# Attention, gated MLP and output projection in one kernel: PV products two at a time in the Wo part, Wo matmuls in blocks of two steps, and other first steps

## The chip, the cores and the metric

The kernel runs on one core of a Trainium2 chip. The metric is the time of the device in microseconds (us); a time is the median of its runs, and next to it stands one profiled execution, from which every duration below is taken. A core has a tensor engine (PE for its matmuls, PEld for its weight loads, which overlap the matmuls), a vector engine (DVE), a scalar engine (ACT), GpSimd (POOL), and SyncE (SP), which issues nearly all DMA transfers here.

## The reference

One block with 2048 tokens of 512 features, an attention with 32 heads of 16 features, and an MLP of width 1376 whose result is the gate of the attention's output:

```python
xn = layernorm(x)                                   # (1, 2048, 512)
q, k, v = split(xn @ wqkv)                          # 32 heads, 16 wide
p = softmax(q k^T / 4)
s = (p v) @ wo
g = silu(gelu_tanh(xn @ w1 + b1) @ w2 + b2)
out = x + s * g
```

## The kernel before

The kernel has three parts. The first, up to about 470 us, makes the layernorm, the transposes, q, k and v and the MLP, each float32 product as three matmuls of split operands; between these matmuls it makes the first 580 of 2048 score tiles that only serve the row maximum ("S tiles"). The second part, which the change touches, is a loop of steps n = 0 to 512. The third, from about 1531 us to the end, makes the Wo product of the last six token tiles.

A step belongs to a unit (four heads by 512 queries; 32 units of 16 steps, so that a step is one unit by 128 keys). It consists of

- four T tiles (`t_one`, L713): transposed scores, 128 keys by 512 queries, one per head. Each uses 64 of the array's rows, so two run side by side; they go to four PSUM banks (`ps`, the two halves of `two`, `pst`), and ACT makes their exponentials in three instructions (L716 for `ps`, L718 for both halves of `two`, L716 for `pst`);
- one PV product V (`pv_step`, L784) of the step before: four matmuls on column tiles (128 rows by 32 columns) that the trace shows as eight records. After the 16th of a unit DVE copies the result out (`os`, L791), `o_move` (L804, L807) sends it on, and `o_den` and `o_div` (L813, L816, L822) divide it by the sums;
- up to three S tiles (L192 on PE, then a maximum on DVE, L198), written S for a whole tile and X and Y for the two halves of one that is cut. They use three banks in a ring. `due(n)` says how many S tiles stand by step n: three a step, but two in the first step (k = 0) of the first `FEW` units after the first. When a unit's 64 are done, DVE (L243, L254), POOL (L245, L246) and four small transfers (L275) put its maxima in memory, and `load_mh` (L162) reads them back as rows of the T tiles' operands;
- or, once S is finished (from step `DONE`), two Wo half products H (`w_halves`, L911). Token tiles 0 to 9 go in five pairs (t, t + 1), four steps a pair. H multiplies one 128-row block k of the attention's output by Wo, for both tokens of the pair at once on the upper and the lower 64 rows ("side" tells which token has which half): three matmuls for each token, which run in pairs, the last pair with the low part `ol`.

The letters of a step's order are written out in strings: `ORDER[3]` = "XTSTTYSTV" with three S tiles, `FIRST` for the first step of a unit with three. For H, other work is hooked behind the n-th T tile. A pair's other work is hooked in the same way: `load_gx` (L840, L841, on SP) loads g and x of a token to one of four `gx` buffers, or to freed places; `w_two` makes the high and low parts of two 128-row blocks of both tokens (ACT L889 high, the very first on POOL L891; POOL L892 low); `gate` is a tanh on ACT (L845) and a product on DVE (L846); `w_out` multiplies the Wo result by the gate (DVE L917), adds x on POOL (L922) and issues the store on SP (L923).

Of the kernel before, what the change touches and what calls it, by code (L numbers as in the profile page):

```python
# [19 lines left out]
H = 32  # L20
# [12 lines left out]
LEAD = 144  # L33
NW = 10
EARLY = 4
DONE = 492
FILL0 = 30
APART = 5
HB = 4
W2B = 2  # L40
ORDER = {0: "TTTTV", 2: "TSTTSTV", 3: "XTSTTYSTV"}
FIRST = "SXTTTSYTV"
SOON = 580
FEW = 4
SIDES = ((1, 1), (0, 0), (0, 1), (1, 0))
HC = CH // 2
PAIRED = 26
# [6 lines left out]
def fused(ctx: ExitStack, tc: tile.TileContext, x, wqk, wv, wo, w1, b1, w2, b2, out):  # L54
    nc = tc.nc
# [47 lines left out]
    def s_tile(held=False):  # L103
        pool = s_ring.pop(0)
        if not held:
            s_ring.append(pool)
        return pool.tile([P, CH], F32, name="ps"), pool
# [64 lines left out]
    def tick():  # L172
        for e in later:
            e[0] -= 1

    def flush():
        while later and later[0][0] <= 0:
            u = later.pop(0)[1]
            s_send(u)
# [5 lines left out]
    def s_mm(ps, job, a, c0, k0, w):  # L185
        u, st, p = job
        qi, ki = at_of(job)
        if u not in MX:
            MX[u] = qring.tile([P, GH, NCH, NCH, 2], F32, name="mx")
        r = slice(64 * a, 64 * a + 3 * DH)  # L190
        k0 += ki * CH
        return nc.tensor.matmul(ps[:, c0:c0 + w], QS[u][r, p, qi * P:(qi + 1) * P],  # L192
                                kts[u // NCH % KB][p][r, k0:k0 + w], start=True, stop=True).ins

    def s_max(ps, job, heads, parts):
        u, p = job[0], job[2]
        qi, ki = at_of(job)
        nc.vector.tensor_reduce(MX[u][:, 2 * p:2 * p + 2, qi, ki][:, heads, parts], ps.rearrange("p (n c) -> p n c", c=HC), axis=AX.X, op=OP.max)  # L198
        done[u] += 1
        if done[u] == 64:  # L200
            ended.append(u)
            if u == NU - 1:
                s_end0(u)

    def s_whole(job, a):
        ps = s_tile()[0]
        s_mm(ps, job, a, 0, 0, CH)
        s_max(ps, job, a, slice(0, 2))
# [7 lines left out]
    def s_op(op):  # L216
        if op == "S":
            if whole:
                s_whole(whole.pop(), 1)
            else:  # L220
                whole.append(jobs.pop(0))
                s_whole(whole[0], 0)
        elif op == "X":
            if not cut:
                cut[:] = [jobs.pop(0), 0]
            ps, pool = s_tile(True)
            x = s_mm(ps, cut[0], 0, 0, cut[1] * HC, HC)
            cut[2:] = [ps, pool, x]
        else:
            job, n, ps, pool, x = cut  # L230
            hold = nc.tensor.nop().ins
            tc.add_manual_dep(hold, x.name, SYNC, reason="row tile done")
            s_mm(ps, job, 1, HC, n * HC, HC)
            s_max(ps, job, slice(0, 2), n)
            s_ring.append(pool)
            cut[1] += 1
            if n:
                cut.clear()

    def s_turn(u, nm):  # L240
        later.append([8 if u == NU - 1 else 12, u])
        nt = qring.tile([P, 2 * GH * NCH], F32, name="nt")
        nc.vector.transpose(nt, nm)  # L243
        mh = MH[u] = qring.tile([P, 2, 2 * GH * NCH], F32R, name="mh")
        nc.gpsimd.tensor_copy(mh[:, 0], nt)  # L245
        nc.gpsimd.tensor_sub(mh[:, 1], nt, mh[:, 0].bitcast(F32))  # L246

    def s_end0(u):
        ended.remove(u)
        us = units_of(u)  # L250
        w = u % 2 * GH * NCH
        nm = nms[u // 2 % 2]
        mx = MX.pop(u).rearrange("p a b c n -> p (a b) (c n)")
        nc.vector.tensor_reduce(nm[:, w:w + GH * NCH], mx, axis=AX.X, op=OP.max, negate=True)  # L254
        if u == us[-1]:
            if "seen" in prog or u == NU - 1:
                s_turn(us[0], nm)
            else:
                put_off.append((us[0], nm))
        del QS[u]  # L260
        if "seen" in prog:
            ask_qs(u + 2)
        else:
            load_qs(u + 2)
# [45 lines left out]
    for j in range(len(pairs)):  # L310
        for h in range(2):
# [9 lines left out]
            n = 2 if nd < len(parts) and parts[nd][2] and ready - nd > room else 1  # L321
            n = max(n, need - 2 * (left - 1))
            while nd < ready and n > 0:
                c, f, k = parts[nd]
# [453 lines left out]
    def pv_step(u, k):  # L778
        g = u // NCH
        if k == 0:  # L780
            PV[u] = ps_v.tile([P, CH], F32, name="pv")
        for j in range(GH):
            h = (g * GH + j) * VW
            nc.tensor.matmul(PV[u][32 * j:32 * j + 32, :], vsb[:, k, h:h + 32], PT[u, k][:, j, :],  # L784
                             start=(k == 0), stop=(k == NT - 1))
        del PT[u, k]
        if k == NT - 1:
            OS[u] = wb.tile([P, CH], F32, name="os", bufs=1)
            pv = PV.pop(u)
            if u < NU - 1:  # L790
                nc.vector.tensor_copy(OS[u], pv)  # L791
            else:
                nc.scalar.activation(OS[u][:, :HC], pv[:, :HC], AF.Copy)
                nc.vector.tensor_copy(OS[u][:, HC:], pv[:, HC:])
# [104 lines left out]
    def w_halves(t, k, side):  # L899
        ts = (t, t + 1)  # L900
        if k == 0 and side == 0:
            for i in ts:
                PW[i] = [s_tile()[0]]
        elif k % 2 == 0:
            hold = nc.tensor.nop().ins
            tc.add_manual_dep(hold, HALF[0].name, SYNC, reason="row tile done")
        for n, (x, y) in enumerate(((0, 0), (0, 1), (1, 0))):
            for a in range(2):
                i = ts[a ^ side]
                r = slice(64 * a, 64 * a + 64)  # L910
                HALF[0] = nc.tensor.matmul(PW[i][0], OTS[i, k][x][r], (wo_h, wo_l)[y][r, k],  # L911
                                           start=k == 0 and side == 0 and n == 0,
                                           stop=k == KT - 1 and side == 1 and n == 2).ins
# [15 lines left out]
    todo = {}  # L929

    def at(n, f, *a, pos=3):
        todo.setdefault((n, pos), []).append((f, a))
# [4 lines left out]
    def due(n):  # L937
        return min(4 * L, SOON + max(0, 3 * n - 1) - min(FEW, n // 16))

# [21 lines left out]
    for t in range(NW):  # L961
        n = DONE + 4 * (t // 2)
        at(n - 3 + t % 2, load_gx, t)
        if t % 2 == 0:
            for i in range(4):
                if i % 2 == 0:
                    at(n + i - 2, w_two, t, i)
                for j in range(2):
                    at(n + i, w_halves, t, i // 2 * 2 + j, i % 2, pos=1 + 2 * j)
        at(n + t % 2, gate, t)  # L970
        at(n + 3, w_out, t, nc.gpsimd)
    for i, t in enumerate(late):
        n = L - 2 * len(late) - 1 + 2 * i
        at(n - 4, load_gx, t)
# [9 lines left out]
    for n in range(L + 1):  # L984
        ua, ka = divmod(n, 16)
        want = due(n) - due(n - 1)
        i = 0
        if put_off and ka > 1:
            s_turn(*put_off.pop(0))
        else:  # L990
            for u in list(ended):
                if u >= PAIRED or ka > 2 and since.setdefault(u, n) < n:
                    s_end0(u)
        order = ORDER[want] if n > 1 else ("TTTTV", "TSTTSVT")[n]
        if want == 3 and ka == 0:
            order = FIRST
        for op in order:
            if op in "SXY":
                s_op(op)
            elif op == "V":  # L1000
                if n:
                    pv_step(*divmod(n - 1, 16))
                for _ in range(4):
                    tick()
                flush()
            else:
                if EARLY <= 4 * n + i < 4 * L:
                    t_one(ua, ka, i, True)
                for f, args in todo.get((n, i), []):
                    f(*args)  # L1010
                i += 1
# [54 lines left out]
```

## Time and profile before

| | |
|---|---|
| median of three runs | 1554.22 us (1554.19 to 1554.6) |
| the profiled execution | 1554.05 us, span 1552.3 us |
| granted TensorE clock | 1.00 |
| busy: PE, DVE, ACT, POOL | 1544.9, 1415.1, 1214.2, 367.7 us |
| steps with three S tiles (V to V) | 2.01 to 2.02 us each |
| first steps of units with three S tiles | about 1.21 us from V's end to the next V, where another step has 1.02 |
| steps with two H | 3.04 to 3.05 us |
| V of step 491 to V of step 512 (21 steps) | 1467.14 to 1530.07 us |

Busy times are sums over the instructions of an engine; PE's records overlap (two tiles side by side), so its share says that PE always has something, not how much of the array works. A row of the timeline gives start, duration, engine, line, output and input, and the number of instructions that were put together. The gap that counts for a step is that between the starts of two V.

### The profile page before, as it was taken

The page shows a single profiled execution, that of the slowest core. Times are in us where ns is not written, and L with a number is a line of the kernel's source. Part 1 is how long each engine was busy: PE and PEld are TensorE (multiplying, and loading weights), DVE is VectorE, ACT ScalarE, POOL GpSimd, SP SyncE. Part 2 cuts the span into 40 slices and gives each one's busy share as a digit, 9 for nine tenths or more (in the row PEclk, how much of TensorE's full clock was granted, in tenths as well). Part 3 has the DMA queues.
Part 4 walks back from the last instruction along what each step waited for, and adds up shares of the span by engine and source line. Part 5 has one row for each costly group of instructions (what it writes and reads, how often), then busy time and mean ns, then how long its engine had stood idle before and what let it go on. Part 6 is the DMA issues. An engine that isn't in the chain of part 4 may idle for free.

```text
span 1552.3 us, 31308 instructions
## 1 busy us (share of the span) xinstructions
PE 1544.9 (100%) x12242; PEld 926.8 (60%) x12242; DVE 1415.1 (91%) x2295; ACT 1214.2 (78%) x1881; POOL 367.7 (24%) x370
## 2 busy tenths in 40 slices
PE   9999999999999999999999999999999999999999
PEld 8899999999994444444444444444444444444455
DVE  7599999999998999999999999999999999999834
ACT  4333433434339999999999999999999999999984
POOL 4145675765741001001000100100010000000143
PEclk9999999999999999999999999999999999999999
DMA  6625443454422113113311411411041111110153
GB/s 211 154 60 146 129 140 100 145 152 122 130 85 77 44 36 67 30 37 61 66 28 30 70 37 36 69 34 29 23 81 29 33 30 32 41 30 22 48 197 115
DMA packets 78643, 116.83 MB, mean 75 GB/s; under 512 B 28036, under 2 KB 28292, under 8 KB 77320
## 3 DMA queue, kind: packets, MB, share of 16 engines
q1 hardware_dynamic: 74748, 101.89, 23.8%
q0 software_dynamic: 3264, 12.35, 4.7%
q8 instruction: 96, 1.57, 0.4%
q10 hardware_dynamic: 484, 0.60, 0.1%
q14 instruction: 51, 0.42, 0.1%
HBM read 84.35 MB, written 25.97 MB: 71 GB/s over the span
## 4 chain that ended last, share of the span: by engine, by line
PE 98%; DVE 1%; DMA 0%; ACT 0%; issue 0%; DVEq 0%
PE pv L784 33%; PE ps L192 22%; PE ps L582 13%; PE two L713 8%; PE sp L582 5%; PE pst L713 4%; PE ps L713 4%; PE pst L582 3%; PE pv L582 2%; PE ps L911 2%; PE ps L91 1%; PE ps L454 1%; PE pst L91 0%; DVE st L413 0%; PE two L91 0%; DMA xt<-in_x 0%
## 5 line engine op out<-in xcount | busy, mean ns | idle before, releaser
L198 DVE TENSOR_REDUCE mx<-ps 128x2 f32<-128x512 f32 x2048 | 1318.5, 687 | 75.3 <-PE ps L192 25.8
L784 PE MATMUL pv<-slot,vsb 128*32 128x512 f32 x4096 | 545.4, 605 | 0.9 <-DVE os L791 0.9
L718 ACT ACTIVATE slot<-two 128x1024 f32<-128x1024 f32 x511 | 520.4, 1018 | 4.3 <-PE pst L713 3.7
L192 PEld LDWEIGHTS ps<-kt,slot 48*128 48x128 f32 x1364 | 214.2, 185 | 295.8 <-DVE mx L198 285.0
L192 PE MATMUL ps<-kt,slot 48*128 48x256 f32 (+1 forms) x1364 | 374.8, 364 | 0.0
L716 ACT ACTIVATE slot<-ps 128x512 f32<-128x512 f32 x515 | 307.1, 597 | 18.0 <-PE ps L713 6.6
L716 ACT ACTIVATE slot<-pst 128x512 f32<-128x512 f32 x511 | 309.5, 606 | 0.6 <-PE ps L713 0.6
L582 PE MATMUL ps<-slot,w1h 64*128 64x512 f32 x1088 | 222.9, 393 | 0.0
L713 PE MATMUL two<-qt,kt 50*128 50x512 f32 x766 | 202.4, 399 | 0.3 <-DVE gt L642 0.3
L192 PE MATMUL ps<-kt,qz 48*128 48x512 f32 x512 | 202.5, 396 | 0.0
L713 PE MATMUL ps<-qt,kt 50*128 50x512 f32 x387 | 190.4, 494 | 0.0
L192 PEld LDWEIGHTS ps<-slot,slot 48*128 48x128 f32 x594 | 93.7, 184 | 126.3 <-DVE mx L198 121.5
L192 PE MATMUL ps<-slot,slot 48*128 48x256 f32 (+1 forms) x594 | 164.8, 364 | 0.0
L582 PEld LDWEIGHTS ps<-slot,w1h 64*128 64x128 f32 x1088 | 155.0, 186 | 8.8
L784 PEld LDWEIGHTS pv<-slot,vsb 128*32 128x32 f32 x4096 | 80.9, 108 | 131.0 <-issue 121.4
L582 PE MATMUL ps<-slot,w1l 64*128 64x512 f32 x544 | 155.1, 393 | 0.0
L713 PE MATMUL pst<-qt,kt 50*128 50x512 f32 x383 | 154.9, 405 | 0.0
L367 ACT ACTIVATE hg<-ps,b_sb 128x512 f32<-128x512 f32 x44 | 27.9, 684 | 134.7 <-PE ps L582 123.3
L374 POOL TENSOR_TENSOR hl<-hg,hh 128x512 fp32r<-128x512 f32 x76 | 96.8, 1296 | 153.2 <-ACT hh L373 107.4
L713 PEld LDWEIGHTS two<-qt,kt 50*128 50x128 f32 x766 | 114.8, 186 | 2.6 <-DVE gt L642 0.7
L245 POOL CAST mh<-nt 128x32 fp32r<-128x32 f32 x19 | 4.0, 209 | 394.0 <-DVE nt L243 329.3
L192 PEld LDWEIGHTS ps<-kt,qz 48*128 48x128 f32 x512 | 93.9, 183 | 0.9 <-DVE mx L198 0.6
(194 smaller groups left out, 1954.5 us busy)
## 6 DMA issues: line engine op xcount, KB each, us to landing
raw<-in_w SPq DMA_DIRECT2D x88, 256.0 KB
qk_h<-hh SPq DMA_DIRECT2D x32, 256.0 KB
qk_l<-hl SPq DMA_DIRECT2D x32, 256.0 KB
qt<-qk_h SPq DMA_DIRECT2D x128, 64.0 KB
slot<-qk_h SPq DMA_DIRECT2D x92, 64.0 KB
g_d<-gt POOLq DMA_DIRECT2D x16, 256.0 KB, 3.6
qt<-qk_l SPq DMA_DIRECT2D x64, 64.0 KB
dn<-den_d SPq DMA_DIRECT2D x32, 128.0 KB
```

The costliest lines, as they stand in the source:

```text
L91: nc.tensor.matmul(ps, lhs[a], rhs[b], start=first and n == 0, stop=last and n == 2)
L192: return nc.tensor.matmul(ps[:, c0:c0 + w], QS[u][r, p, qi * P:(qi + 1) * P], kts[u // NCH % KB][p][r, k0:k0 + w], start=True, stop=True).ins
L198: nc.vector.tensor_reduce(MX[u][:, 2 * p:2 * p + 2, qi, ki][:, heads, parts], ps.rearrange("p (n c) -> p n c", c=HC), axis=AX.X, op=OP.max)
L367: nc.scalar.activation(raw, ph.pop(u), AF.Gelu_apprx_tanh, bias=b1_sb[:, u[2]:u[2] + 1])
L374: nc.gpsimd.tensor_sub(hl, raw, hh.bitcast(F32))
L454: nc.tensor.matmul(pq["q", g, c], W1[g][i][:, k * P:(k + 1) * P], (xh, xl)[j][c][:, k], start=n == 0 and k == 0, stop=n == 2 and k == KT - 1)
L582: i = nc.tensor.matmul(ps, lhs[r], rhs[r], start=first, stop=last).ins
L713: nc.tensor.matmul(ps, kts[g % KB][p][r, k * P:(k + 1) * P], QT[u][r, p, :], start=True, stop=True)
L716: nc.scalar.activation(PT[u, k][:, 2 * p + a, :], ps, AF.Exp, scale=SCALE)
L718: nc.scalar.activation(PT[u, k][:, :2], TP["two"], AF.Exp, scale=SCALE)
L784: nc.tensor.matmul(PV[u][32 * j:32 * j + 32, :], vsb[:, k, h:h + 32], PT[u, k][:, j, :], start=(k == 0), stop=(k == NT - 1))
L911: HALF[0] = nc.tensor.matmul(PW[i][0], OTS[i, k][x][r], (wo_h, wo_l)[y][r, k], start=k == 0 and side == 0 and n == 0, stop=k == KT - 1 and ...
```

## The change

In the Wo part the four T tiles of a step now stand together, and so do the H products, and V is made in even steps only, for the two steps before at once. So a block of two steps reads "TTTTHH" and "HTTTTHVV". The order in which H goes through the blocks k and the sides changes: side 0 of all four blocks first, then side 1, so that one PE wait per pair (the `hold` no-op) is left of the three. `w_two` of a pair's first and second half stand two and one step ahead of the pair. `w_out` stands at the letter W. S ends one step later, since `FEW` goes from 4 to 7: the first steps of units 5, 6 and 7 (n = 80, 96, 112) have two S tiles in place of three, and each S tile after that stands up to three tiles later. Wo starts at step 493 and its last H stand in step 512. In the first steps with three S tiles the first T tile stands ahead of X. New line numbers are one higher (L714 for L713 and so on).

```diff
--- before.py
+++ after.py
@@ -33,15 +33,16 @@
 LEAD = 144
 NW = 10
 EARLY = 4
-DONE = 492
+DONE = 493
 FILL0 = 30
 APART = 5
 HB = 4
 W2B = 2
 ORDER = {0: "TTTTV", 2: "TSTTSTV", 3: "XTSTTYSTV"}
-FIRST = "SXTTTSYTV"
+FIRST = "STXTTSYTV"
+TWO = ("HTTTTHWV", "TTTTHHV")
 SOON = 580
-FEW = 4
+FEW = 7
 SIDES = ((1, 1), (0, 0), (0, 1), (1, 0))
 HC = CH // 2
 PAIRED = 26
@@ -901,7 +902,7 @@
         if k == 0 and side == 0:
             for i in ts:
                 PW[i] = [s_tile()[0]]
-        elif k % 2 == 0:
+        elif k == 0:
             hold = nc.tensor.nop().ins
             tc.add_manual_dep(hold, HALF[0].name, SYNC, reason="row tile done")
         for n, (x, y) in enumerate(((0, 0), (0, 1), (1, 0))):
@@ -962,13 +963,13 @@
         n = DONE + 4 * (t // 2)
         at(n - 3 + t % 2, load_gx, t)
         if t % 2 == 0:
+            for i in range(2):
+                at(n + i - 2, w_two, t, 2 * i)
             for i in range(4):
-                if i % 2 == 0:
-                    at(n + i - 2, w_two, t, i)
                 for j in range(2):
-                    at(n + i, w_halves, t, i // 2 * 2 + j, i % 2, pos=1 + 2 * j)
+                    at(n + i, w_halves, t, i % 2 * 2 + j, i // 2, pos="H")
         at(n + t % 2, gate, t)
-        at(n + 3, w_out, t, nc.gpsimd)
+        at(n + 3, w_out, t, nc.gpsimd, pos="W")
     for i, t in enumerate(late):
         n = L - 2 * len(late) - 1 + 2 * i
         at(n - 4, load_gx, t)
@@ -991,15 +992,22 @@
             for u in list(ended):
                 if u >= PAIRED or ka > 2 and since.setdefault(u, n) < n:
                     s_end0(u)
-        order = ORDER[want] if n > 1 else ("TTTTV", "TSTTSVT")[n]
+        order = TWO[n % 2] if n >= DONE else ORDER[want] if n > 1 else ("TTTTV", "TSTTSVT")[n]
         if want == 3 and ka == 0:
             order = FIRST
         for op in order:
             if op in "SXY":
                 s_op(op)
+            elif op == "H":
+                f, args = todo[n, "H"].pop(0)
+                f(*args)
+            elif op == "W":
+                for f, args in todo.get((n, "W"), []):
+                    f(*args)
             elif op == "V":
-                if n:
-                    pv_step(*divmod(n - 1, 16))
+                for v in range(n - 1, n) if n < DONE else range(n - 2, n) if n % 2 == 0 else ():
+                    if v >= 0:
+                        pv_step(*divmod(v, 16))
                 for _ in range(4):
                     tick()
                 flush()
```

On PE, near the start of the Wo part, one step of before reads as follows; `ps<-qt`, `two` and `pst` are T tiles, `ps<-wo_h`, `wo_l` are H, `pv` is V.

```order
L713 MATMUL ps<-qt_617,kt_113 128x512
L713 MATMUL two<-qt_617,kt_113 128x512
L911 MATMUL ps<-wo_h,oh 128x512 x2
L911 MATMUL ps<-wo_l,oh 128x512 x2
L911 MATMUL ps<-wo_h,ol 128x512 x2
L713 MATMUL two<-qt_617,kt_113 128x512
L713 MATMUL pst<-qt_617,kt_113 128x512
L911 MATMUL ps<-wo_h,oh 128x512 x2
L911 MATMUL ps<-wo_l,oh 128x512 x2
L911 MATMUL ps<-wo_h,ol 128x512 x2
L784 MATMUL pv<-slot_20135,vsb 32x512 x4
```

The end of the first block of after (in step 494), whose two V stand together:

```order
L912 MATMUL ps<-wo_h,oh 128x512 x2
L912 MATMUL ps<-wo_l,oh 128x512 x2
L912 MATMUL ps<-wo_h,ol 128x512 x2
L714 MATMUL ps<-qt_617,kt_113 128x512
L714 MATMUL two<-qt_617,kt_113 128x512 x2
L714 MATMUL pst<-qt_617,kt_113 128x512
L912 MATMUL ps<-wo_h,oh 128x512 x2
L912 MATMUL ps<-wo_l,oh 128x512 x2
L912 MATMUL ps<-wo_h,ol 128x512 x2
L785 MATMUL pv<-slot_20116,vsb 32x512 x4
L785 MATMUL pv<-slot_20149,vsb 32x512 x4
L714 MATMUL ps<-qt_617,kt_113 128x512
```

The T tiles are no longer parted by H, and between two groups of V lie the matmuls of two steps.

On PE, in the first step of unit 30 (n = 480), before (128x512 from `slot` is S, 128x256 is X or Y):

```order
L192 MATMUL ps<-kt_113,slot_4446 128x512
L192 MATMUL ps<-kt_113,slot_4446 128x256
L713 MATMUL ps<-qt_617,kt_113 128x512
L713 MATMUL two<-qt_617,kt_113 128x512 x2
L192 MATMUL ps<-kt_113,slot_4446 128x512
L192 MATMUL ps<-kt_113,slot_4446 128x256
L713 MATMUL pst<-qt_617,kt_113 128x512
L784 MATMUL pv<-slot_19776,vsb 32x512 x4
```

And after:

```order
L193 MATMUL ps<-kt_113,slot_4446 128x512
L714 MATMUL ps<-qt_617,kt_113 128x512
L193 MATMUL ps<-kt_113,slot_4446 128x256
L714 MATMUL two<-qt_617,kt_113 128x512 x2
L193 MATMUL ps<-kt_113,slot_4446 128x512
L193 MATMUL ps<-kt_113,slot_4446 128x256
L714 MATMUL pst<-qt_617,kt_113 128x512
L785 MATMUL pv<-slot_19761,vsb 32x512 x4
```

The first T tile changed places with X; the rest stands as it did.

On POOL, over the first pairs of the Wo part, before (`mh` is the last unit's maxima, `ol` a low part, `slot_6843` with `dn` a division, `gx` an addition of `w_out`):

```order
L245 CAST mh<-nt 128x32
L246 TENSOR_TENSOR mh<-nt,mh 128x32
L892 TENSOR_TENSOR ol<-slot_6842,oh 128x512 x2
L822 TENSOR_TENSOR slot_6843<-slot_6843,dn 64x512
L922 TENSOR_TENSOR gx<-gx 128x512 x2
L892 TENSOR_TENSOR ol<-slot_6842,oh 128x512
L892 TENSOR_TENSOR ol<-slot_6843,oh 128x512
L922 TENSOR_TENSOR gx<-gx 128x512 x2
```

And after:

```order
L246 CAST mh<-nt 128x32
L247 TENSOR_TENSOR mh<-nt,mh 128x32
L893 TENSOR_TENSOR ol<-slot_6842,oh 128x512
L823 TENSOR_TENSOR slot_6843<-slot_6843,dn 64x512
L893 TENSOR_TENSOR ol<-slot_6842,oh 128x512 x2
L923 TENSOR_TENSOR gx<-gx 128x512 x2
L893 TENSOR_TENSOR ol<-slot_6843,oh 128x512 x2
L923 TENSOR_TENSOR gx<-gx 128x512 x2
```

The additions of a pair now stand behind both low parts of the next pair, where they stood between them.

## The prediction

> **What bounds the kernel now.** I read the page first: the busy times, then the chain that ended last.
>
> ```profile
> span 1552.3 us, 31308 instructions
> ...
> PE 1544.9 (100%) x12242; PEld 926.8 (60%) x12242; DVE 1415.1 (91%) x2295; ACT 1214.2 (78%) x1881; POOL 367.7 (24%) x370
> ...
> PE 98%; DVE 1%; DMA 0%; ACT 0%; issue 0%; DVEq 0%
> ```
>
> PE carries 98% of the chain, so what shortens PE's sequence of instructions shortens the kernel, as long as no other engine steps in. Which one could is told by the table of windows for the two stretches that the change touches: 100 steps with S tiles, and the Wo part from the V of step 491 to that of step 512. The columns are the window, its length, then busy time of PE, PEld, DVE, ACT, POOL, the clock, the DMA share and GB/s.
>
> ```profile
> 1200.00:1400.00 200.00, 200.00 (x1576) 89.74 (x1576) 190.68 (x318) 196.69 (x296) 9.98 (x16) 1.00 0.13 32
> 1467.16:1530.07 62.91, 62.06 (x490) 32.57 (x490) 24.44 (x33) 56.25 (x90) 27.40 (x22) 1.00 0.51 170
> ```
>
> With S tiles, ACT is busy 196.7 of 200 us and DVE 190.7: three engines close to their limits. In the Wo part ACT has 6.7 us of 62.9 to spare, and DVE and POOL more. What bounds there is PE's own list. The timeline shows one step:
>
> ```profile
> 1492.63 1.07 PE L784 MATMUL pv<-slot,vsb 128*32 128x512 f32 x8
> ...
> 1493.62 0.49 PE L713 MATMUL ps<-qt,kt 50*128 50x512 f32 x1
> ...
> 1493.96 0.40 PE L911 MATMUL ps<-wo_h,oh 64*128 64x512 f32 x2
> ...
> 1494.66 0.39 PE L713 MATMUL two<-qt,kt 50*128 50x512 f32 x1
> ...
> 1494.89 0.39 PE L911 MATMUL ps<-wo_h,oh 64*128 64x512 f32 x2
> ...
> 1495.36 0.39 PE L911 MATMUL ps<-wo_h,ol 64*128 64x512 f32 x2
> ...
> 1495.67 1.06 PE L784 MATMUL pv<-slot,vsb 128*32 128x512 f32 x8
> ```
>
> A pair of side-by-side matmuls takes .233 us (1494.66 to 1494.89; two pairs from 1494.89 to 1495.36). The first pair after a V takes .34 (1493.62 to 1493.96). The V begins .08 after its turn (1495.36 + .233 = 1495.59, begun 1495.67), and the next T comes .99 to 1.00 after the V began. How long a V is when another V follows it is shown at the end, where V of steps 511 and 512 stand together:
>
> ```profile
> 1529.19 2.03 PE L784 MATMUL pv<-slot,vsb 128*32 128x512 f32 x16
> ...
> 1530.07 0.72 PE L784 MATMUL pv<-slot,vsb 128*32 128x512 f32 x4
> ```
>
> The second begins .88 after the first, the nearest row there is, though it is of only one place. By durations it would be .97 (2.03 less the 1.06 of one V), but that holds a wait for the last exponential. So a lone V costs an island of change from row tiles to column tiles and back: .08 in, .115 out (.995 less .88), .10 in the first pair after: .30 us. With .97 it would be .21.
>
> **The parts of the change, with their price.**
>
> *V two at a time.* A step is now .34 + 7 x .233 + .08 + .995 = 3.05, as the trace has it. A block of two has 16 pairs, two V and one island: 16 x .2333 + 2 x .88 + .30 = 5.79, against 6.09. After: step 492 still has three S tiles, 2.01; then from the V of step 492 to the last V of step 512 come nine blocks of 5.79 (the first V of the first counts for the step ahead) and one without T tiles of step 512, two pairs fewer, 5.33. That is 2.01 + 9 x 5.79 + 5.33 = 59.4, against 62.9 of before: -3.5 us. In this difference lies one stall of before, which goes:
>
> ```profile
> 1484.49 1.37 DVE L846 SCALAR_TENSOR_TENSOR gx<-slot,gx 128x512 f32<-128x512 f32 x1 [3.62 <-ACT slot L845]
> ...
> 1485.79 0.68 DVE L791 COPY os<-pv 128x512 f32<-128x512 f32 x1
> ...
> 1486.52 0.64 PE L784 MATMUL pv<-slot,vsb 128*32 128x512 f32 x4 [0.85 <-DVE os L791]
> ```
>
> The copy that frees V's bank stood on DVE behind a gate, and PE waited .85. Now it stands behind the products of a finished pair, whose inputs are long there; late next is nothing that I see. With the .97 for a second V, ten blocks lose .9 of this: -2.6. Upward no row gives more than .30 an island, so -3.5 is that end too, and I take it: .88 is read from starts, which the wait does not touch.
>
> The Trainium skill (TensorEngine Tiling, Tiling Modes) says that a change of the tiling mode, not of the tile alone, drains the engine, and TensorE: Matmul & The Clock Gate, Single matmul latency, gives a warm latency of (398 + N)/2.4 ns, so 166 ns of it are no streaming. By that estimate an island of two switches costs .33 where the rows give .30, and the nine islands fewer would be worth 3.0 rather than 2.7 us. The rows decide.
>
> *T tiles together, ACT.* The exponentials come in bursts now. A step's three exponentials and what lies among them, in the timeline of ACT:
>
> ```profile
> 1466.66 0.60 ACT L716 ACTIVATE slot<-ps 128x512 f32<-128x512 f32 x1
> ...
> 1468.67 0.60 ACT L716 ACTIVATE slot<-ps 128x512 f32<-128x512 f32 x1
> ...
> 1470.54 0.59 ACT L716 ACTIVATE slot<-pst 128x512 f32<-128x512 f32 x1
> 1471.02 0.63 ACT L889 ACTIVATE oh<-slot 128x512 fp32r<-128x512 f32 x1
> ...
> 1471.54 0.63 ACT L845 ACTIVATE slot<-gx 128x512 f32<-128x512 f32 x1
> ...
> 1472.06 0.60 ACT L716 ACTIVATE slot<-ps 128x512 f32<-128x512 f32 x1
> ```
>
> Starts follow each other closer than durations: a step's exponentials take 2.01 from one `ps` to the next with S tiles (1466.66 to 1468.67; 1.9 where ACT does not wait for PE), each extra instruction .52. The fullest block has two steps and three extras: 2 x 2.01 + 3 x .52 = 5.6 at most, under 5.79. No PE time, then, but only .2 us of slack in the worst block.
>
> *Wo one step later, the first split.* The low part of the first pair's second half is the cost that I find. Its high part now stands in step 492, and on POOL its low part stands behind the last unit's maxima:
>
> ```profile
> 1468.14 0.50 PE L713 MATMUL ps<-qt,kt 50*128 50x512 f32 x1
> ...
> 1469.66 0.25 POOL L246 TENSOR_TENSOR mh<-nt,mh 128x32 fp32r<-128x32 f32 x1
> ...
> 1471.73 1.28 POOL L892 TENSOR_TENSOR ol<-slot,oh 128x512 fp32r<-128x512 f32 x1 [1.81 <-ACT oh L889]
> ```
>
> These maxima end 1.77 us after the first T tile that follows the last S tiles (1469.91 less 1468.14). Added the 1.28 and some .2 for the two handovers, the low part is loaded 3.3 after that T tile. PE wants it after four T tiles (.34 + .23), two H (1.40) and two pairs of the third (.47), at 2.44. That is a stall of .87 once; between 0 (if the split gets ahead on POOL) and 1.3. The later pairs have it earlier: a high part begins at the step's end and the low part is wanted some 2.5 us on, with .8 us left.
>
> *FEW 7.* Three first steps lose one S tile and the maxima after move one step. A first step against a normal one, and against the first step of unit 4, which has two S tiles (timeline, V to V):
>
> ```profile
> 1408.89 0.38 PE L192 MATMUL ps<-kt,slot 48*128 48x256 f32 x1
> ...
> 1409.91 1.06 PE L784 MATMUL pv<-slot,vsb 128*32 128x512 f32 x8
> 1410.15 1.28 DVE L198 TENSOR_REDUCE mx<-ps 128x2 f32<-128x512 f32 x2
> ...
> 1410.91 0.50 PE L192 MATMUL ps<-kt,slot 48*128 48x512 f32 x1
> ...
> 1411.10 0.46 PE L713 MATMUL ps<-qt,kt 50*128 50x512 f32 x1
> ...
> 1411.48 0.18 PEld L192 LDWEIGHTS ps<-kt,slot 48*128 48x128 f32 x1
> ...
> 1411.67 0.51 PE L192 MATMUL ps<-kt,slot 48*128 48x512 f32 x2
> ...
> 1412.12 0.64 PE L784 MATMUL pv<-slot,vsb 128*32 128x512 f32 x4
> ...
> 596.33 0.50 PE L713 MATMUL ps<-qt,kt 50*128 50x512 f32 x1
> ...
> 597.34 0.64 PE L784 MATMUL pv<-slot,vsb 128*32 128x512 f32 x4
> ```
>
> Three S tiles: 1410.91 to 1412.12, 1.21; two: 596.33 to 597.34, 1.01. So 3 x .20 = .6, and some .05 in a later step of each unit that has less to catch up, -.8. The three tiles given back are inside the 2.01 of step 492.
>
> *FIRST.* There are 23 first steps with three S tiles left (n = 128 to 480). Now T stands ahead of X: its matmul began .19 after S (1411.10 less 1410.91), where a normal step starts both at once. But the step's end hangs on another wait: the second S needs a bank that DVE frees at 1411.43 (1410.15 + 1.28), and its weights are loaded at 1411.48, .57 into the step, whatever stands ahead. From these weights to their matmul went .19, where an idle array takes about .12; this .07 is what T ahead saves, 23 x .07 = 1.6. Between 0 (DVE bounds all of it) and .19 each, 4.4.
>
> *A step later for S.* From unit 7 on a unit's last S tiles end closer to the step in which its maxima are collected; I take +.3 from DVE's nearly full stretch (190.7 of 200), between 0 and 1.
>
> Sum: -3.5 + .9 - .8 - 1.6 + .3 = -4.7. The profiled execution took 1554.05, so 1549.35; the median of the runs stood .17 over it, which gives 1549.5. About .2%, 3.1 us, is what a measurement of this kernel can tell from no change: faster is below 1551.1, slower above 1557.3.
>
> **Rivals.**
>
> *FIRST saves all of its wait.* Then 4.4 instead of 1.6: 1546.7. For it, the step's total excess over a normal step is just this .19; against it, the DVE row above.
>
> *The main part gives nothing and V little.* The steps with S tiles are also ACT's (196.7 of 200 us), and what PE gains ACT may take back: then the -2.1 of the main part is 0, and with the .97 for a second V the Wo part is -2.6 + .9 = -1.7: 1552.5, no change by the bound above. For it, the busy shares; against it, that a first step lies .19 over ACT's 2.01, so ACT has caught up there.
>
> *Stores and loads fall behind (slower).* The additions on POOL now stand behind both low parts of the next pair, about 4 us later by the order, and the stores with them; the loads of the next `gx` stand on SP behind a store, in a ring of four buffers.
>
> ```profile
> 1498.20 0.88 SPq L923 DMA_DIRECT2D out<-gx  x2
> ...
> 1502.34 0.32 SPq L840 DMA_DIRECT2D gx<-g_d  x1
> ```
>
> From the issue of two stores to the load that takes the freed buffer went 4.1 us. If the load comes after its gate's turn on ACT, the tanh stands ahead of the exponentials, and PE waits for their banks. By adding up the order I find .5 us left for the gate of token 5. If the next four pairs are late by one such 3.3 us wait for landing each (1502.34 less 1499.08), less the .5, that is 4 x 2.8 = 11.2: 1560.7. It decides from 2.5 us of lateness per pair. Against it: DMA is busy for only .51 of that stretch.
>
> The skill names another way to lateness on POOL (SBUF — State Buffer, Who interferes with whom): a DVE instruction with two SBUF inputs contends with a GpSimd instruction that reads SBUF, and the first one blocks the other. The trace agrees on DVE's side: L846 took 1.37 us beside a low part that kept its 1.30. The other way round a low part would come at most .7 late, within the .8 that later pairs have; it adds a little to this case's chance, nothing to the sum.
>
> **How the numbers follow.** The forecast (about -4.7) gets .45; all of FIRST's wait .13; little gain .29; late loads .13. The predicted time is the first's, 1549.5. The range reaches from the second's 1546.7 to 1553.0, just over the third's, and leaves out the fourth. Faster: .45 + .13 and a little of the third, .60. Within .2%: the rest of the third and the milder half of late loads, .30. Slower: .10.
>
> **What would show it.** In the profile after, V to V in the Wo part should be .88 and then 4.91 (5.79 for two); with .97 and 4.91 the lower price holds. PE should wait once for `ol` in step 494, for about .9 us, and no longer for `os`. First steps should read 1.13 to 1.15 from S to V; 1.21 means that DVE binds them, 1.02 that the wait was all. The last S maximum should end in the step ahead of the first one without S, as before, and one step later in number. A PE wait on ACT's exponentials in the Wo part, with a tanh on ACT that waited for a DMA in front of it, would show the late loads, and would make the prediction wrong; so would any wait of PE in a step of the main part that the trace of before does not have.

## The result and the profile after

The kernel after takes 1550.81 us (median of 10 runs, 1550.2 to 1551.4) against 1554.42 us of before (median of 10, 1554.02 to 1555.74): ratio 0.9975, 95% interval 0.9967 to 0.9983. The profiled execution took 1550.88 us, with a span of 1549.1; that of before was 1552.3. Its page:

```profile
span 1549.1 us, 31305 instructions
...
PE 1541.8 (100%) x12240; PEld 923.4 (60%) x12240; DVE 1416.0 (91%) x2295; ACT 1211.8 (78%) x1881; POOL 366.4 (24%) x370
...
PE 97%; DMA 1%; DVE 1%; ACT 0%; SPq 0%; POOL 0%; issue 0%; DVEq 0%; POOLq 0%
```

DMA, 0% of the chain before, has 1% now. Where the time went is read from the starts of V, in both traces (V 490 is the one that step 491 makes):

| stretch | before, us | after, us | difference | forecast |
|---|---|---|---|---|
| up to V 0 | 469.62 | 469.50 | -.12 | 0 |
| V 0 to V 490 (steps with S tiles) | 997.52 | 994.86 | -2.66 | -2.1 |
| V 490 to V 511 (Wo part) | 62.93 | 61.70 | -1.23 | -2.6 |
| V 511 to the end (last tokens; called the tail below) | 22.20 | 23.04 | +.84 | 0 |
| span | 1552.3 | 1549.1 | -3.2 | -4.7 |

An undisturbed block of two steps, in PE's timeline after:

```profile
1489.42 1.92 PE L785 MATMUL pv<-slot,vsb 128*32 128x512 f32 x16
...
1495.21 1.50 PE L785 MATMUL pv<-slot,vsb 128*32 128x512 f32 x12
```

From one pair of V to the next it is 1495.21 - 1489.42 = 5.79 us, the forecast figure. V to V is .88 and 4.90 to 4.91 everywhere but in two blocks (and in the last one, where step 512 has no T tiles: 4.43). The first, in steps 493 and 494, has 5.68 instead of 4.91; the one of steps 501 and 502 has 6.39. The second loss is the larger, and the timeline shows it:

```profile
1497.07 0.73 PE L714 MATMUL two<-qt,kt 50*128 50x512 f32 x2
...
1498.79 0.63 ACT L846 ACTIVATE slot<-gx 128x512 f32<-128x512 f32 x1 [2.06 <-DMA gx<-g_d]
1499.33 0.58 ACT L717 ACTIVATE slot<-ps 128x512 f32<-128x512 f32 x1
...
1500.87 0.49 PE L714 MATMUL two<-qt,kt 50*128 50x512 f32 x2 [0.42 <-ACT slot L719]
...
1502.49 1.90 PE L785 MATMUL pv<-slot,vsb 128*32 128x512 f32 x13
```

The tanh of token 5 waited 2.06 us on ACT for its load of g. Behind it stood the exponentials of step 501, whose first T tiles had been started at 1497.07; PE waited for their banks, and the block lost 1.48. Why the load came late is told by SP's timeline:

```profile
1489.08 0.37 SPq L814 DMA_DIRECT2D den_d<-dr  x1
1494.01 0.59 SPq L817 DMA_DIRECT2D dn<-den_d  x1
1494.65 0.45 SPq L841 DMA_DIRECT2D gx<-g_d  x1
```

Unit 30's reading back (L817) is issued only when its denominators have landed, 4.9 us after they were sent, and the load for token 5 stands behind it on SP. Before, the same pause was there, but that load stood ahead of it, in SP's timeline of before:

```profile
1491.68 0.43 SPq L840 DMA_DIRECT2D gx<-g_d  x1
...
1492.70 1.29 SPq L813 DMA_DIRECT2D den_d<-dr  x1
1497.52 0.59 SPq L816 DMA_DIRECT2D dn<-den_d  x1
```

The pause was 4.82 us. What moved the load behind it is the start of the Wo part one step later: the load's place counts from that start, the denominators' place from the unit.

The first block's loss is .77, and PE's weight loads after show two waits in it, for the bank of step 493's fourth T tile and for the low part:

```profile
1467.94 0.18 PEld L714 LDWEIGHTS pst<-qt,kt 50*128 50x128 f32 x1 [0.29 <-ACT slot L717]
...
1470.45 0.19 PEld L912 LDWEIGHTS ps<-wo_h,ol 64*128 64x128 f32 x2 [0.59 <-POOL ol L893]
```

### The profile page after: what moved, and what is told of

It is laid out like the page before. It is cut to its first block, busy times and chain, and to the rows that moved or that the text cites. A ratio compares the mean times of both kernels' runs of the same rounds, so it can differ in the third digit from the quotient of the medians.

```text
span 1549.1 us, 31305 instructions
## 1 busy us (share of the span) xinstructions
PE 1541.8 (100%) x12240; PEld 923.4 (60%) x12240; DVE 1416.0 (91%) x2295; ACT 1211.8 (78%) x1881; POOL 366.4 (24%) x370
## 4 chain that ended last, share of the span: by engine, by line
PE 97%; DMA 1%; DVE 1%; ACT 0%; SPq 0%; POOL 0%; issue 0%; DVEq 0%; POOLq 0%
PE pv L785 32%; PE ps L193 22%; PE ps L583 13%; PE two L714 8%; PE sp L583 5%; PE pst L714 4%; PE ps L714 4%; PE pst L583 2%; PE pv L583 2%; PE ps L912 1%; PE ps L455 1%; PE ps L92 1%; PE pv L487 1%; DMA den_d<-dr 0%; DMA dn<-den_d 0%; DMA gx<-g_d 0%
## 5 line engine op out<-in xcount | busy, mean ns | idle before, releaser
L719 ACT ACTIVATE slot<-two 128x1024 f32<-128x1024 f32 x511 | 520.1, 1018 | 0.1
L714 PE MATMUL two<-qt,kt 50*128 50x512 f32 x766 | 198.3, 395 | 0.7 <-ACT slot L719 0.4
L714 PE MATMUL ps<-qt,kt 50*128 50x512 f32 x387 | 189.9, 492 | 0.1
L714 PE MATMUL pst<-qt,kt 50*128 50x512 f32 x383 | 156.0, 407 | 0.0
L714 PEld LDWEIGHTS two<-qt,kt 50*128 50x128 f32 x766 | 115.2, 185 | 1.8 <-ACT slot L719 0.7
```

The costliest lines, as they stand in the source:

```text
L714: nc.tensor.matmul(ps, kts[g % KB][p][r, k * P:(k + 1) * P], QT[u][r, p, :], start=True, stop=True)
L719: nc.scalar.activation(PT[u, k][:, :2], TP["two"], AF.Exp, scale=SCALE)
```

## The experiments

Each kernel was compared with the kernel before in its own session; V to V times are from its profiled execution.

**Only the main part's share.** The kernel before, with these edits:

```diff
-DONE = 492
+DONE = 493
-FIRST = "SXTTTSYTV"
+FIRST = "STXTTSYTV"
-FEW = 4
+FEW = 7
```

> The kernel before with only the main part's share of the change: FIRST, FEW and DONE as after, Wo part as before. Theory of the sum: the steps with S tiles gain 2.7 us, as the V of steps 0 to 490 show in the trace after (-2.79 less -0.12 at the loop's start), and the Wo part stays at 62.9 us from V 490 to V 511: 1554.4 - 2.7 = 1551.7, ratio about 0.9983. Rival: the S tiles given back in step 492 push the old Wo part, whose first pair then starts a step later with the same waits, and the gain is lost there: 1554.4, ratio 1.000.

Measured 1552.45 us against 1554.4, ratio 0.9988 (0.9979 to 0.9997). V 0 to V 490 took 994.79 us, -2.7 as in the kernel after. V 490 to V 511 took 62.68 us, .25 less than before, although step 492 now has three S tiles. There the stall for `os` is gone, too, with no V made in twos: the shift of one step was enough to bring the copy ahead of the gate. The load for token 5 stands behind unit 30's reading back here as well, but its tanh waits for nothing: the shift alone does not make the load late, only the shift with the new order of the Wo part. The median shows 1.95 and not the 2.7 that I expected. In the profiled execution the tail was 23.42, 1.2 us longer than before, and V 0 came .74 later; as it is the longest of the ten, how much of this the median holds is not known.

**Only the Wo part.** The kernel after, with

```diff
-FIRST = "STXTTSYTV"
+FIRST = "SXTTTSYTV"
-FEW = 7
+FEW = 4
```

> The kernel after with FIRST and FEW as before (step 492 has no S tiles then): only the Wo part is changed. Theory of the sum: V 490 to V 511 takes 61.6 us against 62.9, by blocks of 5.79, one stall of .8 for the first pair's low part and one of 1.5 in the block of steps 501 and 502; with a tail as long as after (23.0 from V 511 to the end, against 22.2) that is 1554.4 - 1.3 + .8 = 1553.9, ratio 0.9997. Rival: the longer tail is chance of that execution, and the whole 1.3 us shows: 1553.1, ratio 0.9992. Rival: the late load came from the earlier arrival of the Wo part, and is not there: 1552.4.

Measured 1552.58 against 1554.4, ratio 0.9986 (0.9977 to 0.9996). The time is near the third value, but not for its reason: V 490 to V 511 took 61.33, the block of steps 501 and 502 still lost 1.01 and the first block .88. The late load is there without the main part's gain, with a smaller loss; the reading back is issued 4.41 us after the denominators and not 4.93. The tail was 22.62.

**One V a step, T and H in the new order.**

```diff
-                for v in range(n - 1, n) if n < DONE else range(n - 2, n) if n % 2 == 0 else ():
+                for v in range(n - 1, n):
```

> The kernel after with one V in each step again, T tiles and H products in the same order as after. Theory of islands (.30 for each change to column tiles and back): V to V in undisturbed steps sums to 6.09 for two steps against 5.79, ten islands more, +3.0; the stall of the late load may shrink by up to 1.5, as each block leaves it .3 more: 1552.3 to 1553.8. With .21 an island: 6.00 for two steps, 1551.4 to 1552.9. Rival: the gain comes from T tiles that stand together, not from V: 5.79 for two steps as after, 1550.8.

Measured 1553.31 against 1554.4, ratio 0.9992 (0.9982 to 1.0001). PE's timeline:

```profile
1484.94 1.06 PE L785 MATMUL pv<-slot,vsb 128*32 128x512 f32 x8
...
1488.00 1.06 PE L785 MATMUL pv<-slot,vsb 128*32 128x512 f32 x8
...
1491.07 1.07 PE L785 MATMUL pv<-slot,vsb 128*32 128x512 f32 x8
```

An undisturbed step takes 3.05 to 3.07, two 6.11 to 6.13, where the doubled V has 5.79. T tiles that stand together give nothing by themselves; the doubling of V gives .32 to .34 a block. The late load is here too, with a loss of .7 instead of 1.48; the reading back is issued 3.89 us after the denominators.

**Token 5's load ahead of the denominators.** The kernel after, with

```diff
-        at(n - 3 + t % 2, load_gx, t)
+        at(n - 3, load_gx, t)
```

> The kernel after with the second token's g and x loaded one step earlier, so that on SP the loads of token 5 stand ahead of unit 30's denominators, as they did before the change. Theory: the stall in the block of steps 501 and 502 (7.28 us from V 501 to V 503 instead of 5.79) is the tanh of token 5, which waits on ACT for that load: the block falls to 5.79, 1550.8 - 1.5 = 1549.3, ratio about 0.9967 to before. Rival: the load waits for the gx buffer that an earlier store frees, or for bandwidth, not for its place on SP: the block stays near 7.28, 1550.8. Rival: unit 30's division becomes late in its place, and PE waits for it: a stall elsewhere in steps 503 to 509.

Measured 1549.27 against 1554.4, ratio 0.9966 (0.9953 to 0.9979). The load is issued at 1489.03 instead of 1494.65, the tanh waits for nothing, and the block is 4.91 and .88 like the others:

```profile
1489.03 0.43 SPq L841 DMA_DIRECT2D gx<-g_d  x1
...
1490.04 0.37 SPq L814 DMA_DIRECT2D den_d<-dr  x1
1495.18 0.59 SPq L817 DMA_DIRECT2D dn<-den_d  x1
```

V 490 to V 511 fell from 61.70 to 60.22 by 1.48, the whole stall. Neither buffer nor bandwidth had held the load; its place on SP had. The reading back is issued 1.2 us later, and PE has no wait for it. Where the load keeps its place, the loss goes with the pause from the denominators to their reading back: 1.48 us at 4.93 (1.54 in the next kernel), 1.01 at 4.41, .89 at 4.29 (the kernel with first steps in the order of the others, below), .7 at 3.89.

**The first pair's second split one step earlier.** The kernel after, with

```diff
-                at(n + i - 2, w_two, t, 2 * i)
+                at(n + (i if t else 0) - 2, w_two, t, 2 * i)
```

> The kernel after with the split of the first pair's second half one step earlier (step 491), so that on POOL its low part stands ahead of the last unit's maxima; the loads stay as after. Theory: the first block (5.68 us from V 491 to V 492, where 4.91 is undisturbed) loses its whole wait of .77: 1550.8 - .8 = 1550.0, and the stall of the late load stays. Rival: the maxima come later by the low part's 1.3 us, the loads of the last unit's operands with them, and PE waits at step 496 instead: V 495 to 496 grows, 1550.8 or more. Rival: the wait was not POOL's but one for the exponential of step 492, which stands in front of it: the block stays at 5.4 or more.

Measured 1550.54 against 1554.2, ratio 0.9974 (0.9964 to 0.9985). My theory fell: the first block is 5.63, not 4.91, although its low part is ready in time. The next kernel shows what took its place.

**Both repairs.**

> The kernel after with both repairs, the loads of token 5 ahead of unit 30's denominators and the split of the first pair's second half in step 491. If the two stalls are independent: 1550.8 - 1.5 - .8 = 1548.5, ratio about 0.9962, and V 490 to V 511 is 59.4 us as the sum of blocks says. If the earlier start of the Wo part brings the next load too late: a stall of up to .8 in another block, 1549.3.

Measured 1549.83 against 1554.2, ratio 0.9971 (0.996 to 0.9982); V 490 to V 511 is 60.18, with the late load gone and the first block at 5.64, so neither of the two times expected came. PE's weight loads of the first T tiles of step 493, in the kernel with both repairs:

```profile
1467.80 0.18 PEld L714 LDWEIGHTS ps<-qt,kt 50*128 50x128 f32 x1 [0.84 <-ACT slot L717]
1468.29 0.19 PEld L714 LDWEIGHTS two<-qt,kt 50*128 50x128 f32 x2 [0.30 <-ACT slot L719]
1468.77 0.18 PEld L714 LDWEIGHTS pst<-qt,kt 50*128 50x128 f32 x1 [0.30 <-ACT slot L717]
```

Two waits of .30 for exponentials. The high part (L890) now stands on ACT between the exponentials of steps 491 and 492, where ACT has no time left, and what the four T tiles of step 493 need for their banks comes .4 us later: the second exponential (L719) begins .39 after V, where in the kernel after it begins .02 after it. The .84 of the first row is a V's time and no wait.

**The high part on POOL.** Both repairs, and

```diff
-        if t or k0:
+        if t:
```

> Both repairs, and the high part of the first pair's second half is made on POOL, as that of its first half is, not on ACT. In the kernel with both repairs PE waited .30 twice for exponentials in the first T tiles of step 493, because that high part had put ACT .5 us back in steps that fill it. Theory: without it on ACT the first block (5.64 from V 491 to V 492) falls by about .5 to 5.15, since one wait of about .25 for the bank of the fourth T tile stays; V 490 to V 511 goes from 60.2 to 59.7, and the time to 1548.8 to 1549.3. Rival: POOL is late with four such instructions in a row, and PE waits for the low part as in the kernel after: 5.6 and no gain.

Measured 1548.8 against 1554.79, ratio 0.9963 (0.995 to 0.9975). The first block falls to 5.25, V 490 to V 511 to 59.81. One wait is left, in the weight loads of that kernel:

```profile
1468.01 0.20 PEld L714 LDWEIGHTS two<-qt,kt 50*128 50x128 f32 x2
1468.50 0.18 PEld L714 LDWEIGHTS pst<-qt,kt 50*128 50x128 f32 x1 [0.28 <-ACT slot L717]
```

So a part of the first block's loss is ACT's: with both repairs and nothing added to ACT, .34 of it is left, the wait for the exponential of step 492. In the kernel after, this wait and the low part stand one behind the other: .29 for the fourth T tile's bank, then the low part, whose weights PE awaited for .59.

**First steps in the order of the other steps.** The kernel after, with

```diff
-FIRST = "STXTTSYTV"
+FIRST = "XTSTTYSTV"
```

> The kernel after with FIRST equal to the order of the other steps, XTSTTYSTV. Theory: in the first steps the second S waits for its bank until .53 us after the step's start whatever stands ahead, and what stands behind it decides: with Y ahead of it, not behind, the first step falls from 2.12 to 2.02 us; of the .10 some comes back in the third step, where the copy of the finished unit stands on DVE. As the first change of .10 came back by .025, a gain of .05 to .08 in 23 units: 1549.0 to 1549.7. Rival: the copy on DVE comes later by the order and PE waits for it by as much or more: 1550.8 to 1553.

Measured 1552.9 against 1554.2, ratio 0.9992 (0.9983 to 1.0001): a loss of some 2 us to the kernel after. Over 23 units the mean first step is 2.016, as forecast (2.118 after, 2.214 before), but the second step grows from 2.013 to 2.172 and the third from 2.164 to 2.224. At the start of unit 29, in the timeline of this kernel:

```profile
1413.85 0.68 DVE L792 COPY os<-pv 128x512 f32<-128x512 f32 x1
1414.45 1.88 DVE L199 TENSOR_REDUCE mx<-ps 128x2 f32<-128x512 f32 x3
1414.58 0.16 PEld L785 LDWEIGHTS pv<-slot,vsb 128*32 128x32 f32 x8 [0.40 <-DVE os L792]
```

DVE's copy of the finished unit stands behind the maxima, and PE waits for V's bank. A normal first step takes .16 back in the second step and .06 in the third, more than its .10. The change's .096 per first step is itself paid back by .025 in the third step.

**Stores of tokens 8 and 9 out of the way.** The tail hangs on a chain of small transfers: unit 31's denominators are stored (L814), read back (L817), and divide the last block (L823), from which the last Wo products come. In the kernel after:

```profile
1530.72 0.33 SPq L814 DMA_DIRECT2D den_d<-dr  x1
...
1532.94 0.58 SPq L817 DMA_DIRECT2D dn<-den_d  x1
...
1537.66 0.69 DVE L823 TENSOR_TENSOR ot<-ot,dn 64x512 f32<-64x512 f32 x1 [2.36 <-DMA dn<-den_d]
...
1539.06 0.50 PE L92 MATMUL ps<-wo_h,slot 128*128 128x512 f32 x1 [0.61 <-ACT slot L857]
```

And in the kernel before:

```profile
1535.32 0.33 SPq L813 DMA_DIRECT2D den_d<-dr  x1
1536.73 0.59 SPq L816 DMA_DIRECT2D dn<-den_d  x1
...
1540.85 0.69 DVE L822 TENSOR_TENSOR ot<-ot,dn 64x512 f32<-64x512 f32 x1 [1.39 <-DMA dn<-den_d]
```

From the denominators' issue to the division went 5.5 us before and 6.9 after. A kernel with both repairs was given this edit (and the gate of tokens 8 and 9 stays where `w_out` had it):

```diff
     o_den(NU - 1)
+    for t in (NW - 2, NW - 1):
+        w_add(t, nc.gpsimd)
     w_out(late[0], nc.vector)
```

> As the last one (both repairs), and the additions and stores of tokens 8 and 9 stand behind unit 31's denominators. Theory: the tail is longer after the change (23.0 us from V 511 to the end against 22.2, with 22.6, 23.0 and 22.6 in others) because the small store of the denominators shares the way with two stores of 256 KB issued 2 us ahead of it, so that its reading back is issued 1.9 to 2.3 us later and not 1.4: it falls to 1.4, the tail to 22.2 to 22.4, .2 to .6 under the kernel with both repairs. Rival: these times change from run to run, or the reading back itself is slow: the tail is 22.5 to 23 as there, no difference.

Measured 1549.34 against 1554.2, ratio 0.9968 (0.9956 to 0.9979), and a tail of 22.63 where 22.2 to 22.4 was expected. The reading back is issued 1.74 us after the denominators, not 1.4, and the division comes 9.7 us after V 511, where the kernel with both repairs has 11.4. But PE now waited for POOL, whose additions had taken the place ahead of a low part:

```profile
1531.80 3.44 POOL L923 TENSOR_TENSOR gx<-gx 128x512 f32<-128x512 f32 x2
...
1535.20 1.73 POOL L858 TENSOR_TENSOR ol<-ot,oh 128x512 fp32r<-128x512 f32 x1
...
1536.99 0.50 PE L92 MATMUL ps<-wo_h,ol 128*128 128x512 f32 x1 [0.47 <-POOL ol L858]
```

**The additions behind that low part.** The kernel with the high part on POOL, the gate of tokens 8 and 9 as in the last one, and the two `w_add` lines behind `w_chunk(2, nc.gpsimd)`:

```diff
     w_chunk(2, nc.gpsimd)
+    for t in (NW - 2, NW - 1):
+        w_add(t, nc.gpsimd)
```

> As the last one, and the additions and stores of tokens 8 and 9 stand behind the low part of the last tokens' third block on POOL. In the kernel where they stood ahead of it, the reading back was issued 6.1 us after V 511 and the division came at 9.7 rather than 11.1, but PE waited .8 for that low part. Theory: no wait for POOL and none for the division, the tail from V 511 falls from 22.6 to 22.9 to 22.1 to 22.3: .4 to .6 less than the last one. Rival: the stores of tokens 8 and 9 come so late that they end the kernel, or the tail has another floor: no difference.

Measured 1547.95 against 1554.79, ratio 0.9958 (0.9944 to 0.9971); V 490 to V 511 is 59.81, the tail 22.01, PE waits for nobody in it. This is the fastest of the kernels, 2.9 us under the 1550.81 of the kernel after, though not measured beside it.

**Step 493 with H between the T tiles.** As the last one, and

```diff
+        order = "TTHTTHV" if n == DONE else ...
```

> As the last one, and step 493 alone has two T tiles, one H, two T tiles, one H, so that the fourth T tile comes .7 us later. Theory: what is left of the first block's wait is the fourth T tile's bank, which the exponential of step 492 frees about .25 too late: the block falls from 5.15 to 4.9. Rival: the tiles of step 494 then wait for ACT, since step 493's exponentials start later: no change in the sum of the first block.

Measured 1548.47 against 1554.79, ratio 0.9959 (0.9947 to 0.9972). The first block is 5.15, .11 less than in the kernel of the same session without it; the wait has not gone, as the theory said, nor stayed as it was: PE waits .18 for the fourth T tile's bank, now in step 494, as the rival said. The tail is the same code as in the last kernel, yet 22.94 instead of 22.01:

```profile
1530.33 0.58 SPq L817 DMA_DIRECT2D dn<-den_d  x1
...
1534.68 1.74 DVE L823 TENSOR_TENSOR ot<-ot,dn 64x512 f32<-64x512 f32 x1 [1.22 <-DMA dn<-den_d]
```

From the reading back's issue to the division went 4.35 us here and 3.57 there, and the division took 1.74 rather than 1.23, beside POOL's additions. A single profiled tail can therefore be .9 us off with no change in its code.

All thirteen traces tell where a tail's length comes from. PE's weight loads for the last block's Wo products wait for ACT (L857, L856 in kernels with the line numbers of before), whose input the division gives. This wait was .12 before and 1.05 after, 1.41 with the main part alone, and none in the kernel whose additions stand behind the low part. In twelve traces the tail less this wait is 21.98 to 22.08 us; the thirteenth is the one in which PE waited for POOL. It grew by .93 with the change, so the tail's .84 lies in it.

## Why the prediction was right, and where it was not

The forecast was 1549.5 in a range of 1546.7 to 1553.0, faster; measured was 1550.81, faster by the bound of 1551.1 that the forecast had set. Direction and most terms hold, but two costs that the sum has at nothing came, the late load with 1.48 and the tail with .84, and that the main part gave .6 more than forecast made up for some of it by luck.

- *V two at a time.* Right to the hundredth: 5.79 for a block, .88 for a second V, and nine islands of about .30. The one-V kernel with the same order of T and H shows that the doubling does it, with .32 to .34 a block. The lower price of .97, taken from durations, was wrong. The estimate from the Trainium skill (TensorE: Matmul & The Clock Gate, Single matmul latency), which it gives for one bf16 matmul on the whole array, was .33 an island; the runs do not tell it from my .30.
- *The stall for `os`.* It went, as said. That it goes by the shift of one step alone (the main-part kernel shows it) was not seen.
- *First split.* Size right (.77 against .87), cause half right. I had laid all of it on POOL. Taking POOL out moved .04 to .05 of it only, because the high part, in another step, delayed ACT's exponentials, and .34 stays with neither on ACT nor on POOL. I had checked ACT by sums over blocks and not at the edge from S steps, where it has no slack; the term "no PE time" for ACT failed there.
- *FEW.* The first steps of units 5 to 7 take 2.00 instead of 2.21; from V 64 to V 126 the change gained .82, forecast .8.
- *FIRST.* The 22 whole units with such a first step (8 to 29) gained .075 each (32.592 to 32.517 us a unit), forecast .07: right in sum, and the row on which it rested held: the second S's weights are loaded .58 into the step in both kernels. Its matmul now starts with them, .19 earlier, and the matmul behind it takes .10 more. From S to V a first step reads 1.12, where I had said 1.13 to 1.15. The parts of the gain are -.096 in the first step and +.025 in the third.
- *A step later for S, +.3.* Nothing of it showed; with FIRST's stretch a little better than said (1.86 from V 126 to V 490, where 1.6 was forecast), it is why the main part gave 2.66 and not 2.1.
- *Late loads.* The step that failed. I had named this rival, with token 5's gate as the place and a slack of .5 us, and had given it .13 of the chances and zero in the sum. By the sign that I had set, a PE wait on ACT's exponentials behind a tanh that waited for a DMA, the prediction is wrong here. It came once, for 1.48 us, not in four pairs, and not in the way described: no buffer and no late addition on POOL held the load, since the same load could be issued at 1489.03. It stood behind unit 30's reading back. The sum behind the .5 does not stand in the prediction, so which of its parts was off is open; that the reading back comes 4.8 us after its denominators was to be read in the trace of before. Moving that load alone gave back the whole 1.48. The later pairs were never late.
- *The tail.* The prediction has no term for it, which puts it at nothing. It was .84 longer in the profiled execution, all of it PE's longer wait for the chain behind the division. The same wait varied in the other kernels, from none to 1.41; the pause from denominators to reading back was 1.41 before and 1.68 to 2.33 in the twelve others, so a part may belong to the change. How much is not settled.

So -4.7 of forecast plus 1.48 for the load and .84 for the tail, less .6 of main part, .1 of first split and .1 at the start, is about -3.2, the measured change of the span.

## What to carry to other kernels

A change between row tiles and column tiles on PE has a price that can be read as the difference between a lone V's step and two V in a row; putting such groups together pays it once: here .32 to .34 us for two steps. A block that removes PE time brings every transfer's deadline nearer, so that each queue has to be gone through for what now stands behind a wait, above all a small read that waits for a small store: its time cannot be taken as usual. And one instruction more on an engine that is full at a stage's edge can cost most of its time there, even if the stage has room: the high part, .52 on ACT, cost the first block .39 (5.64 with it, 5.25 without).

## What was not expected of the hardware

A store of 8 KB (unit 30's denominators) and the read that waits for it lay 4.82 us apart before and 4.93 after, from issue to issue, with several loads of 256 KB issued just ahead of it; for units 26 to 29 it was 1.43 to 1.49. That these loads are the reason was not tested, and unit 19's took 10.03 in the trace of after.

Two-operand work on DVE and POOL held each other up: DVE's division took .69 us alone and 1.10, 1.23 and 1.74 while POOL added; a POOL low part took 1.73 rather than 1.28 beside DVE. The ends show how. Each of the three divisions ended .55 after the POOL addition that had begun ahead of it, and that low part 1.14 after the division that had begun ahead of it. In the traces of before and after, from the Wo part on, it is .55 for each DVE instruction with both inputs in SBUF that began beside a POOL one, and 1.14 to 1.16 the other way round (overlaps of more than .1 us). The product of `w_out`, with one input in PSUM, took no more than .69 beside POOL. The Trainium skill (SBUF — State Buffer, Who interferes with whom) says that such a DVE instruction contends with a GpSimd instruction that reads SBUF, and that the one issued first blocks the other; these numbers agree.
